# Pooled attention in groups of 128 and 16 instead of 72 and 72, tables split on the chip, and mixed planes stored twice

## The chip, the core and the metric

The kernel runs on one core of a Trainium2 chip. The metric is the time of one execution on the device in microseconds, the median of three runs. TensorE (PE in the rows, PEld for its weight loads) multiplies matrices, VectorE (DVE), ScalarE (ACT) and GpSimd (POOL) compute elementwise, and SyncE (SP) and GpSimd issue DMA transfers. All engines run their own list of instructions in order and wait for each other through semaphores.

## What is computed

Inputs are q, k, v of shape 8 x 8 x 576 x 64 (batch, heads, positions, width) and two weight matrices of 512 x 2048 and 2048 x 512.

```python
q_d, k_d, v_d = (x.reshape(B, H, 144, 4, D).mean(axis=3) for x in (q, k, v))
out_d = softmax_attention(q_d, k_d, v_d)                  # 144 groups of 4 positions
out_up = np.repeat(out_d, 4, axis=2)
mask = np.abs(pos[:, None] - pos[None, :]) < 4
out_local = masked_softmax_attention(q, k, v, mask)
x = (out_up + out_local) -> (8, 576, 512)
mixed = np.real(fft(fft(x, axis=1), axis=2))
u = x + mixed
un = (u - mean(u)) / sqrt(var(u) + 1e-6)
out = u + relu(un @ w_ch1) @ w_ch2
```

## The kernel before

**Order.** The kernel writes its order by hand. Each piece of work is put into a list with a due time, `at(t, fn)`; the list is sorted, and each engine gets its instructions in that order. The unit is the planner's own and no time on the chip: a batch is `PACE = 20` units, and the table `AT` holds the offsets of every step. An instruction that waits holds up everything behind it on its engine, and a DMA that waits for its source or its buffer holds up the transfers behind it in the queue of SyncE or GpSimd.

**Stages.** For each of the 8 batches: `Unit` is local attention over five pairs of 64-position windows; `Pooled` is attention over the 144 groups; `Mix` folds the result, multiplies it with the tables of cosines and sines (`seqm` along the positions, `chanm` along the channels) as a real Fourier transform, and stores the mixed planes in device memory (`um`). The pooled result goes to `ud`, the local one to `ul`. After the batches comes the feed-forward part: `Block` n takes 512 tokens, adds `ul`, `um` and `ud` into `ut`, normalises, transposes and multiplies with the weights (lines L832 and L850 to L852). The first blocks begin while the last batches are still in work. fp32r products are made from a high and a low part of an operand, three matmuls for one.

**Pooled attention before.** The 144 groups are two halves of 72 on 72 partitions (`GH`). A batch goes in four rounds of two heads; each round has the steps scores (`sp`, L322), maxima (`mxd`, L327), exponentials (`sd`, L338), transposes of 72x72 (`tp`, L348), copies out of PSUM (`ptd`, L359), values (`avd`, L367) and result (`odt`, L378 to L382). `sums` holds the summed q and k (L436 to L439), made from the loaded `qkT` (L419), of which there are six buffers for the five units of a batch. `vsum`, the sums of v, is loaded and then added to three times by DMA (L311). `move` (L391, L392) carries rows of the second half to where the fold wants them: 8 rows inside `odt` and 64 rows to the local result's slot 2; `store` writes `ud`.

**Tables and planes before.** `seqm` and `chanm` come from device memory as high and low part, one DMA each from GpSimd (L552, L555). The mixed planes are two per batch; a block adds them with one DMA for each half of the channels (L762). In `Mix`, `split_low` makes the low part of the folded input on GpSimd (`fl`, L600).

Of the kernel before, what the change touches and what calls it, by code (L numbers as in the profile page):

```python
# [19 lines left out]
POOL_BATCHES = (2,3,4,5,6,7)  # L20
EARLY_LOW = 1

# [8 lines left out]
    "sums": (-2.2, 0.17),  # L31
    "sum_v": (-14.47, -9.55, -2.25, 2.08),
    "load_v": (-2.02, 4.21),
    "store_pooled": (0.1, 0.68),
    "crosses": ((1, 4.04), (2, 6.77), (0, 9.29)),
    "folds": ((3, 4.1), (1, 4.66), (2, 8.37), (0, 10.52)),
    "splits": (0.74, 0.9, 1.86),
    "z": (9.34, 11.56, 13.39, 16.53),
    "sequence": (12.84, 1.74, 0.82, 1.64),
    "mixed": (21.92, 2.32, 0.48, 0.57, 1.73, 2.55),  # L40
    "store_local": (9.77,),
    "ffn": (2.28, 1.64),
    "decode": (49.28, 9.87, 4.65, 1.15, 1.87),
    "decode_steps": (-1.42, -0.6, 0.89, 2.11, 2.34),
    "add0": (61.1, 0.73, 5.8),
    "early": (5.46, 2.11),
    "constants": (17.38, 15.22, 23.31),
    "qk1": (-16.47, 3.41),
    "sum_v1": (-19.42, -12.25, -2.94, 2.36),
    "qk0": (-9.18, 1.93),  # L50
    "sums0": (-0.79, 0.34),
    "sums1": (-1.23, 0.3),
    "load_v0": (1.25, 5.23),
    "load_v1": (0.9, 3.69),
    "sum_v0": (-13.22, -6.45, -4.76, 5.84),
    "pairs0": (4.4, 5.57, 10.95, 11.33),
    "units0": (-2.86, -0.07, 6.22, 12.28, 17.42),
    "norms0": (87.98, -0.75, 94.54, 4.13),
    "add1": (78.83, 3.12, 14.11),
    "norms1": (127.29, 3.89, 1.92, 1.93),  # L60
    "keep": (23.57,),
    "shift": (-0.22,),
    "pace0": (0.95, 1.0),
# [5 lines left out]
ROUND = 5  # L69
TILES = 4  # L70
# [14 lines left out]
def kernel(  # L85
# [24 lines left out]
    GH = G // 2  # L110
# [4 lines left out]
    GX = G - W  # L115
# [14 lines left out]
    um = [dram.tile([2, NSL * P, HN1], F32, name=f"um{b}") for b in range(B)]  # L130
# [101 lines left out]

    odt = pd.tile([GX, 2, DM + 2], F32, name="odt")
    nc.gpsimd.memset(odt[:, :, 0:1], 0.0)
# [38 lines left out]
    for x in xab:  # L273
        nc.gpsimd.memset(x[:, :, :, 0:1], 0.0)
        nc.gpsimd.memset(x[W:, NSL - 1, 1, 1 : DM + 1], 0.0)
# [10 lines left out]
    def pooled_end(b):  # L286
        return pooled_at(b) + (15 if b else AT["pairs0"][3]) + pooled_pace(b) * AT["pooled_steps"][-1]
# [12 lines left out]
    class Pooled:  # L300
        def __init__(self, b):
            self.b = b
            self.sps, self.mx, self.sd, self.tps, self.pts, self.av = {}, {}, {}, {}, {}, {}

        def sum_v(self, r):

            if r == 0:
                self.vs = pd.tile([GH, 2, H, D + 1], F32, name="vsum", bufs=2)
            eng = nc.gpsimd if r else nc.sync
            how = {"accum_op": ALU.add} if r else {}  # L310
            eng.dma_start(out=self.vs.rearrange("g t h d -> g (t h d)"), in_=vg[self.b, r], **how)  # L311

        def scores(self, h0):
            s = sums[self.b]
            sps = self.sps[h0] = [
                bank("sp", GH)[:, : 2 * G].rearrange("p (a g) -> p a g", a=2) for _ in range(2)
            ]
            for t in range(2):
                for hl, sp in enumerate(sps):
                    r = slice(hl * D, hl * D + D)  # L320
                    qT = s[r, 0, h0 // 2, t * GH : (t + 1) * GH]
                    nc.tensor.matmul(sp[:, t, :], qT, s[r, 1, h0 // 2, :], start=True, stop=True)  # L322

        def maxima(self, h0):
            mx = self.mx[h0] = pd.tile([GH, 4], F32, name="mxd", bufs=2)
            for hl, sp in enumerate(self.sps[h0]):
                nc.vector.tensor_reduce(  # L327
                    out=mx[:, 2 * hl : 2 * hl + 2], in_=sp, axis=AX.X, op=ALU.max, negate=True
                )

        def exps(self, h0):
            mx = self.mx[h0]
            nc.scalar.mul(out=mx, in_=mx, mul=2.0**-7)
            sd = self.sd[h0] = pd.tile([GH, 4, G], F32, name="sd", bufs=1)
            for hl, sp in enumerate(self.sps[h0]):
                for t in range(2):
                    i = 2 * hl + t
                    nc.scalar.activation(  # L338
                        out=sd[:, i, :], in_=sp[:, t, :], func=AF.Exp, scale=2.0**-7, bias=mx[:, i : i + 1]
                    )  # L340

        def transpose_p(self, h0):
            self.tps[h0] = []
            for hl in range(2):
                tp = bank("tp", GH)[:, : 2 * G].rearrange("p (a g) -> p a g", a=2)
                for kt in range(2):
                    for t in range(2):
                        nc.tensor.transpose(  # L348
                            tp[:, kt, t * GH : (t + 1) * GH],
                            self.sd[h0][:, 2 * hl + t, kt * GH : (kt + 1) * GH],  # L350
                            ident[:GH, :GH],
                        )
                self.tps[h0].append(tp)

        def copy_p(self, h0):
            self.pts[h0] = []
            for tp in self.tps[h0]:
                pt = pd.tile([GH, 2, G], F32, name="ptd", bufs=NUM_PT)
                nc.scalar.copy(out=pt, in_=tp)  # L359
                self.pts[h0].append(pt)  # L360

        def values(self, h0):
            av = self.av[h0] = bank("avd", GH)[:, : 4 * (D + 1)].rearrange("p (t h d) -> p t h d", t=2, h=2)
            for hl in range(2):
                for t in range(2):
                    for kt in range(2):
                        nc.tensor.matmul(  # L367
                            av[:, t, hl, :],
                            self.pts[h0][hl][:, kt, t * GH : (t + 1) * GH],
                            self.vs[:, kt, h0 + hl, :],  # L370
                            start=(kt == 0),
                            stop=(kt == 1),
                        )

        def result(self, h0):
            av = self.av[h0]
            rs = pd.tile([GH, 2, 2], F32, name="rsd", bufs=2)
            nc.vector.tensor_scalar(  # L378
                out=rs, in0=av[:, :, :, D], scalar1=1e-9, scalar2=4.0, op0=ALU.add, op1=ALU.mult
            )  # L380
            nc.vector.reciprocal(out=rs, in_=rs)
            nc.vector.tensor_mul(  # L382
                out=odt[:GH, :, h0 * D + 1 : (h0 + 2) * D + 1].rearrange("g t (h d) -> g t h d", h=2),
                in0=av[:, :, :, 0:D],
# [742 lines left out]
```

## Time and profile before

| | us |
|---|---|
| median of three runs | 1140.27 (1137.82 to 1142.56) |
| profiled execution | 1141.05 |
| its span, first to last instruction | 1139.3 |
| TensorE busy | 1087.2 (95%) |
| VectorE busy | 513.5 (45%) |
| ScalarE busy | 352.2 (31%) |
| GpSimd busy | 348.0 (31%) |

The busy share is a mean over two different parts. Up to about 333 us the batches are in work and all engines take turns; behind that the feed-forward part runs. A view by stretches separates them. The chain that ended last follows the work back from the last instruction, at each step to what released it.

### The profile page before, as it was taken

The page shows a single profiled execution, that of the slowest core. Times are in us where ns is not written, and L with a number is a line of the kernel's source. Part 1 is how long each engine was busy: PE and PEld are TensorE (multiplying, and loading weights), DVE is VectorE, ACT ScalarE, POOL GpSimd, SP SyncE. Part 2 cuts the span into 40 slices and gives each one's busy share as a digit, 9 for nine tenths or more (in the row PEclk, how much of TensorE's full clock was granted, in tenths as well). Part 3 has the DMA queues.
Part 4 walks back from the last instruction along what each step waited for, and adds up shares of the span by engine and source line. Part 5 has one row for each costly group of instructions (what it writes and reads, how often), then busy time and mean ns, then how long its engine had stood idle before and what let it go on. Part 6 is the DMA issues. An engine that isn't in the chain of part 4 may idle for free.

```text
span 1139.3 us, 20899 instructions
## 1 busy us (share of the span) xinstructions
PE 1087.2 (95%) x8252; PEld 910.8 (80%) x8252; DVE 513.5 (45%) x1230; ACT 352.2 (31%) x1057; POOL 348.0 (31%) x509
## 2 busy tenths in 40 slices
PE   6899797999999899999999999999999999999998
PEld 4787686788978687888888888888888888888887
DVE  4877788779769887132322222222232222132111
ACT  4777565767744443111111111111111111111110
POOL 2346857645364564405003004102201300400000
PEclk7899798889999999999999999999999999999999
DMA  8968989977354442706106005203302401500001
GB/s 265 305 165 259 260 195 261 224 207 201 120 171 125 120 129 66 148 1 131 17 1 134 15 1 111 38 1 97 52 1 78 71 1 56 93 1 34 4 1 37
DMA packets 64195, 119.45 MB, mean 105 GB/s; under 512 B 8573, under 2 KB 22669, under 8 KB 63842
## 3 DMA queue, kind: packets, MB, share of 16 engines
q1 hardware_dynamic: 44850, 87.57, 24.4%
q0 software_dynamic: 19248, 30.56, 15.8%
q8 instruction: 65, 1.06, 0.4%
q14 instruction: 32, 0.26, 0.1%
HBM read 89.86 MB, written 27.05 MB: 103 GB/s over the span
## 4 chain that ended last, share of the span: by engine, by line
PE 73%; DVE 9%; DMA 7%; ACT 5%; POOL 3%; issue 2%; SPq 0%; DVEq 0%; ACTq 0%; POOLq 0%
PE hps L832 30%; PE acc L852 10%; PE acc L850 10%; PE acc L851 10%; DMA raw<-in_wq_dram 3%; DMA qkT<-in_qk_dram 3%; PE y L620 3%; PE mix L666 2%; ACT sb L473 1%; PE avd L367 1%; DVE sums L439 1%; DVE x L521 1%; PE tpn L800 1%; PE av L502 1%; PE sc L454 1%
## 5 line engine op out<-in xcount | busy, mean ns | idle before, releaser
L840 DVE SCALAR_TENSOR_TENSOR hl<-hps,hh 128x512 fp32r<-128x512 f32 x144 | 99.5, 691 | 481.1 <-ACT hh L836 481.1
L832 PE MATMUL hps<-unT,w1h 128*128 128x512 f32 x1152 | 311.1, 392 | 0.0
L832 PEld LDWEIGHTS hps<-unT,w1h 128*128 128x128 f32 x1152 | 214.2, 188 | 43.2
L836 ACT ACTIVATE hh<-hps 128x512 fp32r<-128x512 f32 x144 | 86.0, 597 | 523.6 <-PE hps L832 523.6
L850 PE MATMUL acc<-w2h,hh 128*128 128x512 f32 x576 | 225.5, 391 | 3.1 <-DVE ut L856 2.9
L852 PE MATMUL acc<-w2h,hl 128*128 128x512 f32 x576 | 225.3, 391 | 0.0
L851 PE MATMUL acc<-w2l,hh 128*128 128x512 f32 x576 | 224.6, 390 | 0.0
L832 PE MATMUL hps<-unT,w1l 128*128 128x512 f32 x576 | 154.3, 390 | 0.0
L762 POOL DMA_DIRECT2D ut<-um x96 | 84.1, 1518 | 205.6 <-DMA ut<-ul 172.6
L850 PEld LDWEIGHTS acc<-w2h,hh 128*128 128x128 f32 x576 | 108.4, 188 | 27.1 <-ACT w1h L211 2.0
L852 PEld LDWEIGHTS acc<-w2h,hl 128*128 128x128 f32 x576 | 108.5, 188 | 23.9 <-DVE hl L840 1.3
L832 PEld LDWEIGHTS hps<-unT,w1l 128*128 128x128 f32 x576 | 108.2, 188 | 23.0
L851 PEld LDWEIGHTS acc<-w2l,hh 128*128 128x128 f32 x576 | 108.4, 188 | 22.2
L785 POOL TENSOR_TENSOR rstd<-rstd,mhalf 128x1 f32<-128x1 f32 x36 | 20.1, 558 | 267.5 <-DVE rstd L784 261.7
L473 ACT ACTIVATE sb<-sc,mx 128x64 f32<-128x64 f32 x320 | 70.0, 330 | 1.3
L600 POOL TENSOR_TENSOR fl<-xeo,fh 128x512 fp32r<-128x512 f32 (+1 forms) x32 | 44.1, 1386 | 25.1 <-ACT fh L593 20.2
L809 DVE TENSOR_TENSOR unT<-tpn,unT 128x512 fp32r<-128x512 f32 x36 | 24.8, 690 | 59.0 <-ACT unT L806 59.0
L620 PE MATMUL y<-seqm,fh 128*128 128x290 f32 (+1 forms) x256 | 44.6, 315 | 5.7 <-ACT fh L593 4.2
L181 ACT ACTIVATE wt<-raw 128x256 f32<-128x256 f32 x64 | 28.2, 441 | 64.7 <-DMA raw<-in_wq_dram 47.5
L575 POOL TENSOR_TENSOR pq<-x 128x256 f32<-128x256 f32 x48 | 30.6, 671 | 56.6 <-DVE x L521 47.7
L759 POOL DMA_DIRECT2D ut<-ud x40 | 46.1, 1911 | 2.0 <-DMA ut<-um 1.1
L620 PEld LDWEIGHTS y<-seqm,fh 128*128 128x128 f32 (+1 forms) x256 | 37.4, 197 | 8.8 <-ACT fh L593 5.2
(97 smaller groups left out, 1346.4 us busy)
## 6 DMA issues: line engine op xcount, KB each, us to landing
qkT<-in_qk_dram SPq DMA_DIRECT2D x40, 512.0 KB
raw<-in_wq_dram SPq DMA_DIRECT2D x64, 256.0 KB
vaug<-in_vw_dram SPq DMA_DIRECT2D x40, 260.0 KB
out_dram<-ut SPq DMA_DIRECT2D x36, 256.0 KB
ul<-x SPq DMA_DIRECT2D x8, 1024.0 KB
ut<-ud POOLq DMA_DIRECT2D x32, 256.0 KB, 6.5
vsum<-in_vg_dram POOLq DMA_DIRECT2D x24, 292.5 KB, 7.1
ut<-um POOLq DMA_DIRECT2D x48, 128.0 KB, 4.4
```

The source lines that it names most:

```text
L473: nc.scalar.activation(out=self.sb[:, hp, h2], in_=sc[:, hp], func=AF.Exp, scale=0.125, bias=self.mx[:, h2, hp : hp + 1],)
L575: nc.gpsimd.tensor_tensor(out=pq[:, i], in0=u[:, t, HD + 1 : DM + 1], in1=v[:, t, 0:HD], op=ALU.add)
L600: nc.gpsimd.tensor_sub(out=l, in0=self.x[t], in1=h.bitcast(F32))
L620: nc.tensor.matmul(y, l, r, start=(i == 0), stop=(i == len(mms) - 1))
L759: nc.gpsimd.dma_start(out=u[to : to + m], in_=groups, accum_op=ALU.add)
L762: nc.gpsimd.dma_start(out=u[to : to + m, h * HD : h * HD + HD], in_=um[b][i, k + j : k + j + m, z : z + HD], accum_op=ALU.add,)
L832: nc.tensor.matmul(hps, a[:, c, :], unT[:, x, c, :], start=(i == 0), stop=(i == len(mms) - 1))
L836: nc.scalar.activation(out=hh, in_=self.hps[f], func=AF.Relu)
L840: nc.vector.scalar_tensor_tensor(out=hl, in0=self.hps[f], scalar=0.0, in1=self.hh[f].bitcast(F32), op0=ALU.max, op1=ALU.subtract)
L850: nc.tensor.matmul(acc, hh, w2h, start=start, stop=False)
L851: nc.tensor.matmul(acc, hh, w2l, start=False, stop=False)
L852: nc.tensor.matmul(acc, hl, w2h, start=False, stop=stop)
```

## The change

Pooled attention works on 128 groups and 16 left over. A batch has three parts: part 0 takes the 16 left over of all eight heads at once, as 32-row strips (16 of them other groups that are computed again), parts 1 and 2 take the 128 groups of four heads each. The sums of v carry two more columns of heads with the rows left over, and `spread` copies them on ScalarE into `vds`, zero elsewhere. The result of the 128 groups lies where the fold reads it; the 16 rows left over go to slot 2 of the local result by four small DMAs, and from there to `ud`.

The tables come as plain words in eight pieces through SyncE, into the still unused `ut` tiles; ScalarE makes the high part and VectorE the low part. For batches 0 and 1 three planes are stored, one of them twice, so that one DMA adds both halves of the channels. The low part of fold slot 0 and two small operations of `split_z` go from GpSimd to VectorE. Nearly every offset of the order is another; the lines below show those of the steps named here.

```diff
 AT = {
-    "pooled": (1.17, -0.12, -1.81, -2.91, -3.5),
-    "mix": (19.06, 17.6, 18.05),
-    "local_steps": (0, 1.57, 2.24, 4.76, 5.59, 7.9, 9.26),
-    "pooled_steps": (0.66, 1.79, 2.89, 4.92, 5.63, 7.66, 8.86),
-    "qk": (-12.1, 2.19),
-    "sum_v": (-14.47, -9.55, -2.25, 2.08),
-    "store_pooled": (0.1, 0.68),
+    "pooled": (1.39, -0.67, -3.4, -4.0, -3.53),
+    "mix": (18.69, 18.25, 18.08),
+    "local_steps": (0.47, 2.18, 2.55, 4.76, 5.66, 7.44, 8.16),
+    "pooled_steps": (0.21, 1.79, 2.89, 4.92, 5.63, 7.66, 9.61),
+    "qk": (-14.26, 2.19),
+    "sum_v": (-14.82, -12.57, -2.25, 2.01),
+    "store_pooled": (1.06, 1.34, 3.47),
...
-    "constants": (17.38, 15.22, 23.31),
-    "sum_v1": (-19.42, -12.25, -2.94, 2.36),
-    "norms1": (127.29, 3.89, 1.92, 1.93),
-    "shift": (-0.22,),
+    "constants": (10.75, 29.61),
+    "waves": ((16.5, 0.16), (17.55, 0.92), (21.37, 0.9)),
+    "waves_c": ((21.38, -3.88), (23.72, -0.25), (25.94, 6.11)),
+    "sum_v1": (-19.42, -12.25, -4.44, 3.9),
+    "norms1": (146.64, 3.89, 0.79, 1.85),
+    "shift": (0.5,),
+    "parts": (0.22, 5.36, 9.32),
+    "spread": (11.49, 5.0),
...
-    um = [dram.tile([2, NSL * P, HN1], F32, name=f"um{b}") for b in range(B)]
+    um = [dram.tile([4 if b < TWICE else 2, NSL * P, HN1], F32, name=f"um{b}") for b in range(B)]
...
-                self.vs = pd.tile([GH, 2, H, D + 1], F32, name="vsum", bufs=2)
+                self.vs = pd.tile([P, H + 2, D + 1], F32, name="vsum", bufs=2)
...
+        def spread(self):
+            for k in range(4):
+                r = slice(k * LQ, k * LQ + LQ)
+                nc.scalar.copy(out=vds[self.b % 2][r, :, k % 2], in_=self.vs[r, H:])
+
+        def scores(self, i):
...
+            for a in range(2 if i else HP):
+                for hl, sp in enumerate(sps):
+                    r = slice(hl * D, hl * D + D)
+                    if i:
+                        hp = 2 * i - 2 + a
+                        nc.tensor.matmul(sp[:, a, :], s[r, 0, hp, :P], s[r, 1, hp, :], start=True, stop=True)
+                    else:
+                        nc.tensor.matmul(
+                            sp[a * LQ : a * LQ + LQ, 0, :], s[r, 0, a, G - LQ :], s[r, 1, a, :], start=True, stop=True
+                        )
...
+        def transpose_p(self, i):
+            sd, n = self.sd[i], self.sps[i][0].shape[1]
+            main, rest = (bank("tp")[:, : m * P].rearrange("p (m q) -> p m q", q=P) for m in (2 * n, 1))
+            for a in range(n):
+                for hl in range(2):
+                    nc.tensor.transpose(main[:, 2 * a + hl, :], sd[:, a, hl, :P], ident)
+            for k in range(4):
+                x = sd[:, k % 2 if i else 0, k // 2, G - LQ :]
+                nc.tensor.matmul(rest[k * LQ : k * LQ + LQ, 0], x, ident, start=True, stop=True)
...
+        def values(self, i):
...
+            for a in range(1 if i else HP):
+                for hl, o in enumerate(av):
+                    r = slice(hl * D, hl * D + D)
+                    q = slice(0, P) if i else slice(a * LQ, a * LQ + LQ)
+                    v = vd[r, i - 1] if i else vd[r, a // 2, a % 2]
+                    nc.tensor.matmul(
+                        o.rearrange("p a d -> p (a d)") if i else o[q, 0, :],
+                        rest[r, 0, q],
...
+            for a in range(2 if i else HP):
+                for hl, o in enumerate(av):
+                    hp = 2 * i - 2 + a if i else a
+                    q = slice(0, P) if i else slice(a * LQ, a * LQ + LQ)
+                    nc.tensor.matmul(
+                        o[:, a, :] if i else o[q, 0, :],
+                        main[:, 2 * a + hl if i else hl, q],
+                        self.vs[:, 2 * hp + hl, :],
...
         def move(self):
             x = xab[self.b % 2]
-            STORE.dma_start(out=odt[GH:GX, 0, 1 : DM + 1], in_=odt[W:GH, 1, 1 : DM + 1])
-            STORE.dma_start(out=x[W:, NSL - 1, 0, 1 : DM + 1], in_=odt[:W, 1, 1 : DM + 1])
+            for hp in range(HP):
+                STORE.dma_start(
+                    out=x[W : W + GL, NSL - 1, 0, 1 + hp * P : 1 + hp * P + P],
+                    in_=self.rest[(hp + 1) * LQ - GL : (hp + 1) * LQ],
+                )
+
+        def store_rest(self):
+            STORE.dma_start(out=ud[self.b][P:], in_=xab[self.b % 2][W : W + GL, NSL - 1, 0, 1 : DM + 1])
...
-    def sequence_waves():
-        nc.gpsimd.dma_start(out=seqm, in_=c_seq)
...
+    def load_waves(k):
+        nc.sync.dma_start(out=waves[k][1], in_=waves[k][0])
+
+    def waves_high(k):
+        nc.scalar.copy(out=waves[k][2], in_=waves[k][1])
+
+    def waves_low(k):
+        nc.vector.tensor_sub(out=waves[k][3], in0=waves[k][1], in1=waves[k][2].bitcast(F32))
...
-            nc.gpsimd.tensor_sub(out=l, in0=self.x[t], in1=h.bitcast(F32))
+            eng = nc.vector if t in LOW_ON_VECTOR else nc.gpsimd
+            eng.tensor_sub(out=l, in0=self.x[t], in1=h.bitcast(F32))
...
+                elif part and b < TWICE:
...
+                    nc.gpsimd.dma_start(
+                        out=u[to : to + m].rearrange("p (h c) -> p h c", h=2),
+                        in_=planes.rearrange("h (r c) -> r h c", c=HN1)[:, :, :HD],
+                        accum_op=ALU.add,
+                    )
```

## Rows read from the trace of the kernel before

**Rows 1.** Busy us of each engine by stretch, with granted clock, DMA share, GB/s.
```profile
core 0: us, PE busy (x) PEld busy (x) DVE busy (x) ACT busy (x) POOL busy (x), PEclk, DMA share, GB/s
16.00:333.00 317.00, 280.71 (x4550) 245.34 (x4551) 242.46 (x719) 208.19 (x766) 171.11 (x261) 0.91 0.79 219
20.00:40.00 20.00, 19.25 (x391) 15.42 (x388) 15.29 (x47) 13.83 (x55) 5.18 (x7) 0.88 0.97 297
...
400.00:1000.00 600.00, 599.90 (x2690) 495.45 (x2690) 177.55 (x332) 94.81 (x178) 135.65 (x177) 1.00 0.27 59
```

**Rows 2.** Chain that ended last, 16 to 333 us, share of the stretch by line.
```profile
by line: PE y L620 9.1%; DMA qkT<-in_qk_dram 7.6%; ACT sb L473 5.2%; PE avd L367 5.1%; PE mix L666 5.0%; DVE sums L439 4.9%; DVE x L521 4.9%; PE av L502 4.4%; issue 4.1%; PE sc L454 3.5%; PE sp L322 2.9%; PE tpl L485 2.9%; PE tp L348 2.6%; 
```

**Rows 3.** TensorE in order of time: start us, us, engine, line, operation, count.
```profile
281.17 0.60 PE L485 MATMUL tpl<-ident,sb 128*128 128x128 f32 x4
281.60 0.67 PE L348 MATMUL tp<-ident,sd 72*72 72x72 f32 x8
282.20 0.71 PE L322 MATMUL sp<-sums 64*72 64x144 f32 x8
282.84 0.51 PE L666 MATMUL mix<-chanm,yh 128*128 128x258 f32 x2
...
284.27 0.29 PE L666 MATMUL mix<-chanm,yl 128*128 128x258 f32 x1
284.40 0.28 PE L666 MATMUL mix<-signs,yz 128*128 128x258 f32 x1
284.61 0.70 PE L502 MATMUL av<-vaug,pT 64*64 64x65 f32 x32
...
285.80 1.25 PE L367 MATMUL avd<-vsum,ptd 72*72 72x65 f32 x16
286.87 0.43 PE L666 MATMUL mix<-chanm,yh 128*67 128x258 f32 x2
```

**Rows 4.** Chain over the whole span, single pieces: start us, us, what.
```profile
59.45 6.51 DMA qkT<-in_qk_dram
...
81.31 2.15 DMA odt<-odt
...
184.71 8.02 DMA qkT<-in_qk_dram
...
227.57 9.49 DMA qkT<-in_qk_dram
```

**Rows 5.** Chain, 117 to 141.3 us, share of the stretch by line.
```profile
by line: POOL ut L762 28.0%; DMA odt<-odt 13.7%; POOL fl L600 9.1%; PE avd L367 7.8%; ACT sb L473 7.2%; PE mix L666 6.5%; issue 4.6%; PE tpl L485 3.6%; DVE o L678 3.2%; DVE xeo L586 3.1%; PE y L620 2.5%; ACT pT L493 2.4%; ACT fh L593 2.1%; 
```

**Rows 6.** Groups by line and form up to 345 us: count, busy us, mean ns.
```profile
L338 ACT ACTIVATE sd<-sp,mxd 72x144 f32<-72x144 f32 x128 | 37.9, 373 | 1.4 <-PE tp L348 0.4
L600 POOL TENSOR_TENSOR fl<-xeo,fh 128x512 fp32r<-128x512 f32 x24 | 34.1, 1424 | 7.9 <-ACT fh L593 6.7 <-DMA qkT<-in_qk_dram 1.0
...
L327 DVE TENSOR_REDUCE mxd<-sp 72x2 f32<-72x288 f32 x64 | 26.0, 445 | 10.0 <-PE sp L322 10.0
...
L762 POOL DMA_DIRECT2D ut<-um x22 | 20.1, 1362 | 0.3 <-DMA vaug<-in_vw_dram 0.2
...
L809 DVE TENSOR_TENSOR unT<-tpn,unT 128x512 fp32r<-128x512 f32 x5 | 3.4, 686 | 3.8 <-ACT unT L806 3.8
```

**Rows 7.** Chain that ended last, share of the span by engine, from the page.
```profile
PE 73%; DVE 9%; DMA 7%; ACT 5%; POOL 3%; issue 2%; SPq 0%; DVEq 0%; ACTq 0%; POOLq 0%
```

**Rows 8.** Busy time of each engine over the span, from the page.
```profile
PE 1087.2 (95%) x8252; PEld 910.8 (80%) x8252; DVE 513.5 (45%) x1230; ACT 352.2 (31%) x1057; POOL 348.0 (31%) x509
```

**Rows 9.** DMA issues of the tables: KB each, us to landing.
```profile
seqm<-in_c_seq_dram POOLq DMA_DIRECT2D x1, 2320.0 KB, 12.2
...
chanm<-in_c_chan_dram POOLq DMA_DIRECT2D x1, 1032.0 KB, 11.6
```

**Rows 10.** Line L391, the moves: count, duration ns, first and last start us.
```profile
L391 SPq DMA_DIRECT2D odt<-odt x8: 698/704/767, 42.9 to 309.6; - x8
```

**Rows 11.** Line L311, additions of vsum, from issue to landing.
```profile
DMA to landing us min/median/max: 4.7/7.1/11.1
```

More of the change, by code (lines that the diff above doesn't have):

```diff
@@ L231 @@
     pd = p1.enter_context(tc.tile_pool(name="pd", bufs=1, side="right"))
-    odt = pd.tile([GX, 2, DM + 2], F32, name="odt")
-    nc.gpsimd.memset(odt[:, :, 0:1], 0.0)
+    odt = pd.tile([P, DM + 2], F32, name="odt")
+    nc.gpsimd.memset(odt[:, 0:1], 0.0)
+    vds = [pd.tile([P, 2, 2, D + 1], F32, name=f"vd{i}") for i in range(2)]
+    for x in vds:
+        nc.gpsimd.memset(x, 0.0)
     pbank = ExitStack()
@@ L331, in exps @@
[L331 to L373, printed above, removed]
@@ new lines, in result @@
+        def result(self, i):
+            av = self.av[i]
+            n = av[0].shape[1]
+            rs = pd.tile([P, 2, 2], F32, name="rsd", bufs=2)[:, :, :n]
+            for hl, o in enumerate(av):
+                nc.vector.tensor_scalar(
+                    out=rs[:, hl], in0=o[:, :, D], scalar1=1e-9, scalar2=4.0, op0=ALU.add, op1=ALU.mult
+                )
+            nc.vector.reciprocal(out=rs, in_=rs)
+            if i:
+                to = odt[:, 1 + (i - 1) * 4 * D : 1 + i * 4 * D]
+            else:
+                to = self.rest = pd.tile([P, 2 * D], F32, name="rest", bufs=1)
+            to = to.rearrange("p (a h d) -> p a h d", h=2, d=D)
+            for hl, o in enumerate(av):
+                nc.vector.tensor_mul(
+                    out=to[:, :, hl], in0=o[:, :, 0:D], in1=rs[:, hl].unsqueeze(2).to_broadcast([P, n, D])
+                )
@@ L581, in fold @@
             if t < NSL:
-                a, b = self.pq[t][:, 0], self.pq[t][:, 1]
+                a, b = (self.pq[t][: rows[t], i] for i in range(2))
             else:
-                a, b = odt[:, 0, HD + 1 : DM + 1], odt[:, 0, 0:HD]
+                a, b = odt[:, HD + 1 : DM + 1], odt[:, 0:HD]
             nc.vector.tensor_add(out=x[:, 0:HD], in0=a, in1=b)
@@ L594, in split_high @@
             if t == NSL:
-                nc.scalar.copy(out=zf[:n, t], in_=odt[:, 0, HD : HD + 1])
+                nc.scalar.copy(out=zf[:n, t], in_=odt[:, HD : HD + 1])
         def split_low(self, t):
@@ L886 @@
         u.plan()
-    for t, fn in zip(AT["constants"], (sequence_waves, channel_waves, clear_yz)):
+    for t, fn in zip(AT["constants"], (load_signs, clear_yz)):
         at(t, fn)
+    for k in range(len(waves)):
+        for (first, step), fn in zip(AT["waves" if k < 5 else "waves_c"], (load_waves, waves_high, waves_low)):
+            at(first + step * (k if k < 5 else k - 5), fn, k)
     last = mix_at(B - 1)
@@ L1013, in _constants @@
         seq[rows, 1, m // 2] = sn
[L1015 to L1025 removed]
+    g = np.arange(S // 4)
+    g = np.where(g < S // 8, g, S // 4 - 1 - (g - S // 8))
+    group = np.zeros((2, S // 4, len(k1)))
+    for r in range(4):
+        group += np.stack(waves(4 * g + r))
+    seq[:, :, 3] = group[:, :P].transpose(1, 0, 2)
+    seq[W : W + S // 4 - P, :, 2] = group[:, P:].transpose(1, 0, 2)
+    seq = seq.reshape(P, -1)
     j = np.arange(DM // 2 + 2)
```

218 lines of the change are left out of this document (122 added, 96 removed).

## Prediction

> **What bounds the kernel now.** I read the page first, then the busy time by stretch, then the chain that ended last, and last the single rows of the instructions that the change removes or adds. The span is 1139.3 us and the profiled execution took 1141.05, so 1.75 us lie outside the span. From 400 to 1000 us TensorE is busy 599.90 of 600 us at full clock [rows 1]: that is the feed-forward part, which the change does not touch, so it can only start earlier or later. What can move is the 317 us from 16 to 333. There TensorE is busy 280.71 us (89%), VectorE 242.46, ScalarE 208.19, the granted clock averages 0.91 of 2.4 GHz, and the DMA engines are busy 0.79 of the time, 0.97 from 20 to 40 us at 297 GB/s [rows 1]. No engine is full; the work goes from engine to engine. The chain confirms it: in that stretch its largest items are the sequence matmuls (9.1%), the landing of qkT (7.6%), the exponentials (5.2%) and the pooled value matmuls (5.1%) [rows 2]. The reader is to see that an instruction saved is worth its share on the chain, and its whole time only where its engine is what everybody waits for.
>
> **TensorE.** Durations are steps between starts in a stretch that keeps TensorE busy at full clock [rows 3]: four transposes of 128x128 take 0.43 us (0.108 each), eight pooled transposes of 72x72 take 0.60 (0.075), eight pooled scores 0.64 (0.080), sixteen pooled values 1.07 (0.067). A batch has 32, 32 and 64 of them: 2.56 + 2.40 + 4.29 = 9.25 us. After, a batch has 16 score matmuls (8 with 128 stationary columns, 8 with 32), 10 transposes of 128x128, 12 plain matmuls against the identity and 28 value matmuls (12 with 128 stationary columns, 16 with 32). No row shows these shapes. I price the wide ones, the transposes and the plain matmuls as the 128x128 transpose (0.108), the narrow scores at 0.080 and the narrow values at 0.067: scores 0.86 + 0.64, transposes 1.08 + 1.30, values 1.30 + 1.07, together 6.25 us. That saves 3.0 us a batch, 24 us in all. If the narrow ones run four at a time, as the 64x64 local matmuls seem to (32 of them begin and end within 0.70 us), the 24 narrow ones cost about 0.02 each and the plain ones 0.067: 4.5 us a batch, 38 us saved. The low end: the three lines hold 5.1 + 2.9 + 2.6 = 10.6% of the chain's 317 us, 33.6 us [rows 2], of which 3.0/9.25 is 10.9. TensorE is at 89%, so the truth lies between chain share and full price; I take the middle of 10.9 and 24, **-17**.
>
> The new code asks for more kinds of tiles: per part the transposes go from full height to 32-column pieces and the values from half height to full. The row shows what such a step costs: within the mix group one matmul follows another after 0.13 us, the first 64x64 matmul after it comes 0.21 us later [rows 3], so 0.08 more. With 2 more steps a part, 6 a batch, 48 in all, that is about 4 us; at the same share as above (17 of 24) **+3**. The Trainium skill (TensorEngine Tiling (Array Packing), Tiling Modes, Key Properties) says that changing the tiling mode drains TensorE. If a drain is the part of a matmul's record that its successor normally hides, 0.28 - 0.13 = 0.15 us [rows 3], 48 of them are 7.2 us in place of 3, and the sum below would be 4 us worse; the row of 0.08 speaks for less.
>
> **The moved rows.** Before, 8 rows of odt go to itself and 64 rows to x by DMA once the last pair of heads is done, and the fold of the group slot waits for them. On the chain this landing stands twice: 2.15 us [rows 4] and 13.7% of 24.3 = 3.33 us [rows 5]. After, slot 3 is read where the result was written, and the 16 rows left over go out after the first part, two parts before they could hold anything up. What is late next is the fold itself, which waited for nothing else. **-5.5**; at worst the second landing finds another cover and it is -2.
>
> **The mixed planes.** In 117 to 141.3 us the additions of um fill 28.0% of the chain, 6.8 us [rows 5]: GpSimd issues them (1.362 us each, 22 up to 345 us, all of batches 0 and 1 [rows 6]) and the low parts of the sequence input stand behind them. After, one DMA carries both halves, so 11 are issued. If an issue costs as before the half is saved, **-3.4**; if it costs double, because it names twice the pieces, nothing; if the rest moves off the chain too, 6.8.
>
> **VectorE, ScalarE, GpSimd.** VectorE gets the low part of slot 0 (8 at 0.686, the price of a subtraction of that size [rows 6]) 5.5 us, eight table subtractions of at most that price, 5.5, and sixteen tiny z operations, which no row here prices, between nothing and the 0.445 of a 72x288 reduction; I take 0.2, so 3.2. The maxima go from 64 at 0.445 to 32 of that width and 16 of half of it (0.33, between half price and full): 28.5 to 19.5. The normalisations are more but smaller (15 against 12 a batch): nothing. Net +5.2 us. ScalarE loses 48 exponentials at 0.373 [rows 6], 17.9 us; its 8 table copies and 32 spread copies stand against a quarter fewer copies out of PSUM and fewer scalings: nothing net. GpSimd loses 8 subtractions at 1.424 [rows 6], 11.4 us. Shares: the chain spends 9, 5 and 3% of the span on these engines [rows 7], 102.5, 57 and 34 us, over busy times of 513.5, 352.2 and 348.0 [rows 8]: 0.20, 0.16 and 0.10. So +1.0 - 2.9 - 1.1 = **-3.0**.
>
> **Bytes.** The tables were 2320 and 1032 KB [rows 9]; half of that, 1.72 MB, goes away in the stretch in which DMA is full, 5.8 us at 297 GB/s. The group sums of v grow from 292.5 to 325 KB, 32 times, 1.06 MB over the whole stretch; two planes more are 0.6 MB; the moves fall by 0.9 MB. I take **-2**, between 0 and -6.
>
> **Two waits that the new order makes.** A batch is 20 units of the order; the eight moves run from 42.9 to 309.6 us [rows 10], 38.1 us a batch, 1.9 us a unit.
> First, qkT. On the chain its landing takes 6.51, 8.02 and 9.49 us [rows 4]. The load of the next batch's last unit needs the buffer that the local scores of unit 3 free, so it cannot start sooner. From those scores to the next batch's pooled scores the order has 5.16 units (9.8 us) before and 4.21 (8.0 us) after for batches 4 to 7, 5.75 and 3.74 for batch 3, 6.85 and 4.34 for batch 2: 8.3 units, 15.8 us less in all. That bounds the loss from nothing to 15.8; behind the waiting scores stand the local matmuls on TensorE. I take **+5**, as three landings in seven stood on the chain.
> Second, the spread. ScalarE now copies rows of vsum 2.99 units (5.7 us) after its last addition is issued, 1.1 units (2.1 us) in batch 1; the first reader used to come 5.58 units after. An addition lands after 7.1 us in the median, 4.7 at least and 11.1 at most [rows 11]. So 1.4 us in six batches and 5.0 in batch 1, 13.5 us of ScalarE, with the local exponentials and copies queued behind. At ScalarE's share that is 2.2; **+3**. The table copies wait for plain loads issued units earlier; I cost that at nothing, covered by the exponentials before them, and 3 us if the first loads are late.
>
> **Sum.** -17 + 3 - 5.5 - 3.4 - 3.0 - 2 + 5 + 3 = -19.9. From the profiled execution's 1141.05 that is 1121.2; the median of the runs is 0.8 lower, 1140.27, so **1120 us**.
>
> **The rivals.**
> TensorE is the limit after all: clock 0.91 and 89% busy speak for it, the chain's mixed engines against. Then -30 (between 24 and 38) + 3 - 5.5 - 6.8 - 3 - 6 = -48, **1092**.
> The time saved comes back as the wait for qkT: for it, that scores now stand 1 to 2.5 units nearer to the loads; against it, that four batches show no such landing on the chain. With TensorE at its low end and the um DMAs at double price: -10.9 + 3 - 5.5 - 3 - 2 + 3 + 15.8 = +0.4, **1140**, no change; so too if the change simply lies off the path.
> Slower: ScalarE stands at the spread until vsum has landed. If additions land as late as the latest, 11.1 us, six batches stand 5.4 us and batch 1 9.0: 41 us, all on the path because the local exponentials are behind. Against the sum without its +3: -22.9 + 41 = +18, **1158**. It decides from about 3.3 us a batch on (22.9 over 7), that is, when landings come later than 9.0 us; the median of 7.1 speaks against it.
>
> **How the numbers follow.** Chances: the sum 0.55 (own range 1108 to 1133), TensorE the limit 0.13, qkT or off the path 0.19, the spread 0.13. A difference of 0.5% (5.7 us) is about what a measurement of this kernel can tell from none. Faster: 0.55 + 0.13 and 0.02 of the qkT case, 0.70. Same: 0.16 of that case. Slower: the spread's 0.13 and 0.01 of the qkT case, 0.14. The range 1097 to 1145 leaves out most of the case of 1092 (0.09) and of 1158 (0.11).
>
> **What the profile after would show.** Right: the feed-forward part as long as now and starting about 20 us sooner; no landing of odt on the chain; the three pooled TensorE lines down from 10.6% of the stretch to 7; half as many um additions and no stretch like 117 to 141 us; TensorE's idle time in 16 to 333 us not above today's 36 us. Wrong: ScalarE waiting at the spread for vsum by more than 3 us a batch, landings of qkT in every batch, plain identity matmuls well above 0.108 us, or a feed-forward part that starts earlier and then waits for its weights, since their decoding starts only when the local buffers close.

## The result, and the profile after

The kernel after the change takes 1125.43 us (median, 1123.41 to 1127.43) where the one before took 1141.41 in the same comparison: a ratio of 0.9864, interval 0.9832 to 0.9896, so 16 us or 1.4% faster. The forecast was 1120 with a range of 1097 to 1145. The total is close. The experiments show that most of the terms behind it are not.

The profiled execution took 1124.34 us. First the page: the busy time of each engine, and the chain that ended last by engine.

```profile
PE 1065.8 (95%) x8204; PEld 880.6 (78%) x8204; DVE 519.7 (46%) x1270; ACT 349.2 (31%) x1025; POOL 330.5 (29%) x473
...
PE 78%; DMA 8%; DVE 6%; ACT 4%; issue 2%; POOL 1%; SPq 0%; POOLq 0%; ACTq 0%; DVEq 0%
```

Next the busy time by stretch. The columns are those of [rows 1]; 316.72 us is where the first matmul of the second weight matrix starts (line L931, tile `acc`; L850 before, at 328.46).

```profile
16.00:316.72 300.72, 258.98 (x4489) 213.22 (x4490) 243.39 (x752) 201.71 (x729) 149.37 (x219) 0.93 0.81 225
20.00:40.00 20.00, 14.26 (x334) 10.59 (x326) 15.02 (x49) 13.47 (x50) 3.19 (x4) 0.93 0.90 238
140.00:160.00 20.00, 10.23 (x169) 8.40 (x168) 9.96 (x35) 6.62 (x24) 6.20 (x11) 0.74 0.96 239
317.00:389.00 72.00, 69.61 (x329) 57.29 (x328) 64.69 (x131) 33.07 (x84) 41.28 (x66) 1.00 0.44 127
400.00:1000.00 600.00, 600.00 (x2698) 496.49 (x2697) 171.94 (x318) 91.50 (x165) 126.91 (x162) 1.00 0.26 55
```

The same view of before, cut at its own first `acc` matmul:

```profile
16.00:328.46 312.46, 276.18 (x4525) 241.28 (x4526) 238.89 (x710) 205.58 (x758) 168.59 (x257) 0.91 0.80 221
```

That is 312.46 us with TensorE busy 276.18 at a mean granted clock of 0.91. So the span's 16.7 us (1139.3 to 1122.6) fall apart like this: 11.7 us before that matmul and 5.0 after it (810.8 to 805.9). In the first part TensorE is busy 17.2 us less and idle 5.4 us more (41.7 against 36.3). Not all of the 17.2 us is work that is gone, since the same matmuls are busy for longer at a lower clock: the experiment "Only z on GpSimd" below has the same 4489 records and is busy 268.33 us at a mean clock of 0.90. Busy time multiplied by the mean clock is 276.18 x 0.91 = 251 us before and 258.98 x 0.93 = 241 after. By this estimate, good to some 2 us because the clock has two digits, about 10 us are matmuls saved and about 7 are the higher clock. New holes have opened: 20 to 40 us had 19.25 busy [rows 1] and has 14.26; 140 to 160 us has 10.23, at a mean clock of 0.74, so partly at the lower of the two levels, 1.2 GHz.

Of the 5 us behind the first `acc` matmul some 3.5 can be named. Before, 14 sequence matmul records still stood there, now 2: twelve at 0.145 us, 1.7 us. The first 72 us ran at a mean clock of 0.98 and now run at 1.00: 1.4 us. TensorE's idle time from the first `acc` matmul to the end fell from 6.9 to 6.5 us.

The chain from 16 to 318 us, shares by line and then single pieces (start us, us, what), answers to [rows 2, 4, 5].

```profile
by line: DMA raw<-in_wq_dram 11.3%; DMA vsum<-in_vg_dram 8.8%; PE y L686 7.7%; issue 4.9%; ACT sb L525 4.5%; PE mix L732 4.5%; DMA qkT<-in_qk_dram 3.8%; PE tpl L537 3.6%; PE avd L406 3.5%; PE sc L506 2.9%; PE av L554 2.3%; DMA vaug<-in_vw_d
...
21.02 7.06 DMA vsum<-in_vg_dram
...
43.80 5.00 DMA vsum<-in_vg_dram
...
68.61 7.16 DMA vsum<-in_vg_dram
...
100.88 8.41 DMA raw<-in_wq_dram
...
135.54 17.94 DMA raw<-in_wq_dram
...
185.84 7.87 DMA raw<-in_wq_dram
...
219.41 6.89 DMA qkT<-in_qk_dram
```

The reader is to see three things. No landing of `odt` is left, as forecast. The landing of `qkT`, on which the forecast put 5 us, went from 24.0 [rows 4] to 3.8% of 302 = 11.5 us. And the largest item is one that the forecast did not have: the weights' raw words (`raw`), 34.1 us of the chain (11.3%), one piece of it 17.94 us long.

The groups up to 345 us (columns as in [rows 6]):

```profile
L360 ACT ACTIVATE sd<-sp,mxd 128x144 f32<-128x144 f32 x80 | 24.4, 381 | 0.8
...
L836 POOL DMA_DIRECT2D ut<-um x11 | 13.7, 1583 | 0.3
...
L342 PE MATMUL sp<-sums 64*128 64x144 f32 x128 | 12.7, 317 | 0.0
...
L330 ACT COPY vd<-vsum 32x130 f32<-32x130 f32 x32 | 9.5, 298 | 2.3 <-DMA vsum<-in_vg_dram 2.0
...
L666 DVE TENSOR_TENSOR fl<-xeo,fh 128x512 fp32r<-128x512 f32 x8 | 6.5, 815 | 0.8 <-ACT fh L658 0.7
...
L675 DVE TENSOR_TENSOR z<-zf,z 128x4 fp32r<-128x4 f32 x8 | 3.4, 424 | 2.7 <-ACT z L674 2.7
```

The waits from 16 to 318 us (who, for what: us in all, times, longest):

```profile
ACT wt L187 <- DMA raw<-in_wq_dram: 14.7, 5, 8.7
...
ACT z L674 <- DVE zf L671: 5.8, 5, 3.4
...
PE yz L710 <- DVE z L675: 4.8, 4, 2.0
...
ACT vd L330 <- DMA vsum<-in_vg_dram: 2.0, 3, 1.5
```

On VectorE slot 0's low part takes 0.815 us (forecast 0.686) and the subtraction of `split_z` 0.424 (forecast 0.2). The spread, on which the slower rival rested, makes ScalarE wait 2.0 us in all; the forecast had 13.5. The additions of `um` are halved, 22 to 11, at 1.583 us in place of 1.362. The longest wait for raw words and what stands behind it, in order of time:

```profile
153.50 0.43 ACT L187 ACTIVATE wt<-raw 128x256 f32<-128x256 f32 x1 [8.66 <-DMA raw<-in_wq_dram]
...
155.04 0.80 PE L732 MATMUL mix<-chanm,yh 128*128 128x258 f32 x2 [9.09 <-ACT sb L525]
```

ScalarE stands 8.66 us at a word that isn't there; the local exponentials (`sb`, L525) are behind it in its list, and TensorE stands 9.09 us for them. That is the hole at 140 to 160 us.

### The profile page after: what moved, and what is told of

Read it like the earlier page. It is cut to its first block, busy times and chain, and to the rows that moved or that the text cites. A ratio compares the mean times of both kernels' runs of the same rounds, so it can differ in the third digit from the quotient of the medians.

```text
span 1122.6 us, 20797 instructions
## 1 busy us (share of the span) xinstructions
PE 1065.8 (95%) x8204; PEld 880.6 (78%) x8204; DVE 519.7 (46%) x1270; ACT 349.2 (31%) x1025; POOL 330.5 (29%) x473
## 4 chain that ended last, share of the span: by engine, by line
PE 78%; DMA 8%; DVE 6%; ACT 4%; issue 2%; POOL 1%; SPq 0%; POOLq 0%; ACTq 0%; DVEq 0%
PE hps L913 34%; PE acc L931 11%; PE acc L933 11%; PE acc L932 11%; DMA vsum<-in_vg_dram 3%; DMA raw<-in_wq_dram 3%; PE y L686 2%; PE mix L732 2%; ACT sb L525 1%; PE tpn L881 1%; DMA qkT<-in_qk_dram 1%; PE tpl L537 1%; PE avd L406 1%; PE sc L506 1%; PE av L554 1%
## 5 line engine op out<-in xcount | busy, mean ns | idle before, releaser
L931 PE MATMUL acc<-w2h,hh 128*128 128x512 f32 x576 | 224.7, 390 | 2.0 <-DVE ut L937 2.0
L931 PEld LDWEIGHTS acc<-w2h,hh 128*128 128x128 f32 x576 | 108.0, 188 | 25.4 <-DVE ut L937 2.0
L843 POOL DMA_DIRECT2D ut<-um x72 | 62.1, 1538 | 195.7 <-DMA ut<-ul 162.5
L525 ACT ACTIVATE sb<-sc,mx 128x64 f32<-128x64 f32 x320 | 70.0, 330 | 1.3
L732 PE MATMUL mix<-chanm,yh 128*128 128x258 f32 (+1 forms) x160 | 34.4, 310 | 13.8 <-ACT sb L525 11.1
L887 ACT CAST unT<-tpn 128x512 fp32r<-128x512 f32 x36 | 21.2, 588 | 76.8 <-PE tpn L881 76.8
L192 POOL TENSOR_SCALAR wt<-wt 128x256 f32<-128x256 f32 x64 | 31.7, 496 | 35.3 <-ACT mx L522 14.1
L206 DVE SCALAR_TENSOR_TENSOR wt<-raw,wt 128x256 int32<-128x256 int32 x64 | 40.5, 633 | 2.2
```

What stands on the lines that cost most here:

```text
L206: nc.vector.scalar_tensor_tensor(out=t, in0=self.lo, scalar=29, in1=t, op0=ALU.logical_shift_right, op1=ALU.bitwise_or)
L525: nc.scalar.activation(out=self.sb[:, hp, h2], in_=sc[:, hp], func=AF.Exp, scale=0.125, bias=self.mx[:, h2, hp : hp + 1],)
L732: nc.tensor.matmul(to, l, r, start=(i == 0), stop=(i == len(mms) - 1))
L843: nc.gpsimd.dma_start(out=u[to : to + m, h * HD : h * HD + HD], in_=um[b][i, k + j : k + j + m, z : z + HD], accum_op=ALU.add,)
L931: nc.tensor.matmul(acc, hh, w2h, start=start, stop=False)
```

## The experiments

All ratios are to the kernel before, which ran in each comparison again (medians of 1139.18 to 1141.49 us); they can differ by up to 0.0017 from the quotient of the two medians. The first two questions: did the total come from TensorE, and which of the small edits count?

**Planes once** (after, without the doubled planes).

```diff
-TWICE = 2
+TWICE = 0
```

> The changed kernel, with two planes per batch again and two additions for each piece (the order is not touched). Theory A, the parts add up as forecast: 3.4 us slower than the changed kernel (between 0 and 6.8), so about 1129 us, and GpSimd issues 22 additions up to 345 us in place of 11. Theory B, the pooled attention and the order bring everything: within 2 us of the changed kernel, since GpSimd was not what the others waited for.

1125.9 us, 0.986 (0.9838 to 0.9882). The doubled planes can't be told from nothing here, nor from the forecast 3.4 us: a difference below some 4 us lies within these intervals.

**Tables by GpSimd** (after, tables as high and low part again, by one DMA each).

```diff
-        nc.sync.dma_start(out=waves[k][1], in_=waves[k][0])
...
+        nc.gpsimd.dma_start(out=seqm, in_=c_seq)
...
+        nc.gpsimd.dma_start(out=chanm, in_=c_chan)
```

> The changed kernel, with the tables coming as high and low part by one DMA each from GpSimd, at the offsets they had before. Theory A: 1.72 MB more in a stretch in which DMA is full, against 8 pieces less on ScalarE and on VectorE: 1 us slower (between 3 faster and 5 slower). Theory B: within 2 us. A third view: the DMA engines are the limit up to 60 us, then all of 5.8 us comes back, 1131 us.

1126.07 us, 0.986 (0.9838 to 0.9882). The saved bytes can't be told from nothing either.

**Low parts on GpSimd** (after, slot 0's low part and both operations of `split_z` back).

```diff
-LOW_ON_VECTOR = (0,)
+LOW_ON_VECTOR = ()
...
-            nc.vector.tensor_tensor(
+            nc.gpsimd.tensor_tensor(
...
-            nc.vector.tensor_sub(out=z[:, :, 1:2], in0=zf, in1=z[:, :, 0:1].bitcast(F32))
+            nc.gpsimd.tensor_sub(out=z[:, :, 1:2], in0=zf, in1=z[:, :, 0:1].bitcast(F32))
```

> The changed kernel, with the low part of fold slot 0 and the two small z operations on GpSimd again. Theory A: nothing that can be measured, since 11.4 us less on GpSimd at its chain share of 0.10 and 8.7 us more on VectorE at 0.20 cancel. Rival: GpSimd's queue stands in front of the sequence matmuls, then 8 times 0.7 us or more come back, 1131 us or above.

1135.91 us, 0.9956 (0.9933 to 0.998): 10 us lost, the first edit that counts. Its waits from 16 to 333 us offer two causes, `vsum` at the spread and `z` at TensorE:

```profile
ACT vd L330 <- DMA vsum<-in_vg_dram: 11.2, 6, 3.2
...
PE yz L710 <- POOL z L675: 10.2, 6, 2.5
```

**Weights earlier** (after, decoding planned 2 units earlier).

```diff
-    "decode": (50.58, 9.93, 4.05, 1.15, 1.87),
+    "decode": (50.58, 9.93, 6.05, 1.15, 1.87),
```

> The changed kernel, with the fetch of the weight quarters that are decoded during the batches 2 units earlier. Theory D: a wait is new in the changed kernel, ScalarE for the weights' raw words, 18.2 us in all and 8.7 at the longest, with TensorE idle for 9.1 us behind it, because the fetch stands 2.71 units (5 us) ahead of its first reader where it stood 3.23. Then an earlier fetch takes most of it away: 5 to 10 us faster, 1115 to 1120, and no wait of ScalarE for raw above 3 us. Rival: the DMA engines are full there, so the fetch lands as late or something else lands later in its place: within 2 us.

1122.39 us, 0.983 (0.9808 to 0.9852): the lowest median of the study, 3 us below the kernel after, though the two intervals overlap. ScalarE's wait for raw words falls from 14.7 to 4.8 us, the longest from 8.7 to 1.8. But other landings stand on the chain in its place, one of them here:

```profile
144.63 10.81 DMA vsum<-in_vg_dram
```

So the hole is closed in part (from 140 to 160 us TensorE is busy 14.29 us, in place of 10.23) and in part exchanged: the DMA engines are full there in both kernels (share 0.96, now 1.00), the words come sooner, and the sums of v stand on the chain in their place.

**Pooled alone** (the edits of the first three together, so that of the change only the pooled part, the moves and the order stay).

> The changed kernel, with two planes, the tables by GpSimd, and the low part of slot 0 and z on GpSimd, all three at once: what is left of the change is the pooled attention in 128 and 16, and the order. Theory A, the parts add up: 1125.4 + 3.4 + 1 = about 1130 us, 11 faster than before. Theory B, pooled attention and order bring everything: about 1125 us. If the three together hide a loss of the pooled part: 1138 or above.

1139.03 us, 1.0016 (0.9991 to 1.0041). Without the three small edits the change gains nothing. Its busy time by stretch, up to its own first `acc` matmul:

```profile
16.00:327.61 311.61, 270.24 (x4489) 220.51 (x4490) 225.62 (x721) 197.96 (x721) 168.31 (x256) 0.89 0.78 221
```

By the estimate above the matmuls are saved here too (270.24 x 0.89 = 241, as in the kernel after, against 251). A lower clock, 0.89 against 0.91, and 41.4 us of idle time against 36.3 take the saving back.

**Half the values, before** (the kernel before, with the second half of the value matmuls left out).

```diff
-                    for kt in range(2):
...
+                    nc.tensor.matmul(
+                        av[:, t, hl, :],
+                        self.pts[h0][hl][:, 0, t * GH : (t + 1) * GH],
```

> The kernel before, with half of the pooled value matmuls left out (the second half of the groups is not added, so the output is not the reference's): 32 of 64 instructions of 0.067 us a batch, 17 us of TensorE in all, and nothing else changed. It prices a microsecond of TensorE. Chain share: half of the 16.2 us that the line has on the chain, 8 us faster, 1133. TensorE as the limit: 17 us faster, 1124. Others are the limit: within 2 us.

1138.95 us, 0.9998 (0.9978 to 1.0018). Its busy time by stretch, up to its own first `acc` matmul:

```profile
16.00:325.50 309.50, 261.18 (x4269) 223.02 (x4270) 235.32 (x707) 205.85 (x758) 168.43 (x257) 0.91 0.80 223
```

TensorE is busy 15.0 us less than in the same stretch of before (276.18), and idle 12.0 us more (48.3 against 36.3). TensorE's time alone buys nothing in the old order.

**Planes twice, before** (the old kernel with the doubled planes alone).

```diff
-    um = [dram.tile([2, NSL * P, HN1], F32, name=f"um{b}") for b in range(B)]
+    um = [dram.tile([4 if b < TWICE else 2, NSL * P, HN1], F32, name=f"um{b}") for b in range(B)]
```

> The kernel before, with only the three planes of batches 0 and 1 and one addition for both halves. Theory A: 3.4 us faster (between 0 and 6.8), 1138, with the stretch of 117 to 141 us shorter. Theory B: within 2 us, because what stands behind the additions on GpSimd waits for something else next.

1147.62 us, 1.0084 (1.0056 to 1.0111), slower. A landing of `qkT` of 13.93 us stands on the chain where the kernel before had none; whether it is the cause was not tried:

```profile
144.33 13.93 DMA qkT<-in_qk_dram
```

**Scores doubled** (after, each wide pooled score matmul twice; a repeat overwrites the first).

```diff
-                        nc.tensor.matmul(sp[:, a, :], s[r, 0, hp, :P], s[r, 1, hp, :], start=True, stop=True)
+                        for _ in range(2):
+                            nc.tensor.matmul(sp[:, a, :], s[r, 0, hp, :P], s[r, 1, hp, :], start=True, stop=True)
```

> The changed kernel, with the wide pooled score matmuls issued twice (the second writes the same result): 16 instructions of 0.087 us more a batch, 11 us of TensorE in all. TensorE as the limit: 11 us slower, 1136. Chain share: the line has 2.5 us on the chain, so 2 to 4 us slower, 1128 to 1129. Others are the limit: within 2 us.

1129.44 us, 0.9923 (0.9904 to 0.9942), so 0.0059 of 1141, 6.7 us, above the kernel after, for 11 us of matmuls: 0.6 us for each. Saving in the old order gave nothing, adding in the new costs more than half. The price of a microsecond of TensorE depends on what else is late.

**Low parts on VectorE, before** (the reverse of the third experiment, in the old kernel).

```diff
-            nc.gpsimd.tensor_sub(out=l, in0=self.x[t], in1=h.bitcast(F32))
+            eng = nc.gpsimd if t else nc.vector
+            eng.tensor_sub(out=l, in0=self.x[t], in1=h.bitcast(F32))
```

and both operations of `split_z` as in the change.

> The kernel before, with only the low part of fold slot 0 and the two small z operations on VectorE. Putting them back on GpSimd cost the changed kernel 10 us. Theory F: that is so because GpSimd's last addition of vsum stands behind them and ScalarE and TensorE now wait for it at the spread; the kernel before reads vsum 5.58 units after that addition is issued, so it gains little: within 3 us, 1137 to 1143. Rival: GpSimd in front of the sequence matmuls was a bound of the kernel before as well: 7 to 11 us faster, 1129 to 1133.

1150.46 us, 1.007 (1.0043 to 1.0097): 8 us slower. What the new order needs hurts the old one. Its TensorE waits 8.4 us for low parts on VectorE, where the kernel before waits 4.7 for those on GpSimd, and VectorE waits 9.9 us for ScalarE between the two operations of `split_z`; whether these are the cause was not tried.

**Low parts on GpSimd, sums early** (the third experiment again, with the last additions of `vsum` issued sooner, to tell its two waits apart).

```diff
-    "sum_v": (-14.82, -12.57, -2.25, 2.01),
+    "sum_v": (-14.82, -12.57, -7.0, -2.3),
```

> The kernel with the low part of slot 0 and z on GpSimd again (1135.9 us), in which the third and the last addition of vsum are issued 4.75 and 4.31 units earlier, in front of the sums of q and k. Theory F: the 10 us were the wait for vsum at the spread (11.2 us of ScalarE's idle time), so most of it comes back: 1126 to 1130, and ScalarE's idle time at the spread falls below 3 us. Rival: the 10 us are the sequence matmuls' wait for low parts and z on GpSimd, 21 us of idle time before the z matmuls: then 1133 or above.

1137.86 us, 0.9971 (0.9947 to 0.9996). Its waits, 16 to 333 us:

```profile
PE yz L710 <- POOL z L675: 12.8, 6, 4.2
...
ACT vd L330 <- DMA vsum<-in_vg_dram: 1.2, 2, 1.1
```

The wait at the spread went from 11.2 to 1.2 us and the time did not come back: that cause fell. `z` and slot 0's low part are left.

**Only z on GpSimd** (after, only the two operations of `split_z` back; slot 0's low part stays on VectorE).

```diff
-            nc.vector.tensor_tensor(
+            nc.gpsimd.tensor_tensor(
...
-            nc.vector.tensor_sub(out=z[:, :, 1:2], in0=zf, in1=z[:, :, 0:1].bitcast(F32))
+            nc.gpsimd.tensor_sub(out=z[:, :, 1:2], in0=zf, in1=z[:, :, 0:1].bitcast(F32))
```

> The changed kernel, with only the two small z operations on GpSimd, the low part of slot 0 stays on VectorE. Theory F (the low part of 1.4 us in front of the additions of vsum is what costs): within 3 us of the changed kernel. Rival (the z operations wait in GpSimd's queue and TensorE for them): 5 to 10 us slower, 1130 to 1135.

1136.26 us, 0.9946 (0.9925 to 0.9967). The whole loss of the third experiment is in sixteen operations of 0.2 us. One of them in order of time, first GpSimd's list and then TensorE's:

```profile
214.54 1.22 POOL L640 TENSOR_TENSOR pq<-x 128x256 f32<-128x256 f32 x2 [0.75 <-DVE xeo L651]
215.73 0.19 POOL L671 TENSOR_TENSOR zf<-x 128x3 f32<-128x3 f32 x1
216.23 0.20 POOL L675 TENSOR_TENSOR z<-zf,z 128x4 fp32r<-128x4 f32 x1 [0.30 <-ACT z L674]
```

```profile
216.48 1.24 PE L710 MATMUL yz<-seqm,z 128*2 128x290 f32 x8 [1.37 <-POOL z L675]
```

Its waits from 16 to 318 us, and behind them its busy time up to its first `acc` matmul:

```profile
ACT z L674 <- POOL zf L671: 16.7, 8, 4.8
...
PE yz L710 <- POOL z L675: 13.9, 7, 3.4
```

```profile
16.00:328.62 312.62, 268.33 (x4489) 219.32 (x4490) 236.67 (x738) 201.55 (x729) 154.69 (x235) 0.90 0.77 217
```

`z` stands behind the fold's additions (`pq`) on GpSimd, and TensorE waits for it 13.9 us in place of 4.8. ScalarE, which makes the high part of `z`, waits longer too, 16.7 us for `zf` in place of 5.8; the runs don't separate the two waits. The change of order is the likely reason why this matters now, though no run moves it back: in the kernel before, also with `z` on GpSimd, TensorE waits for it only 1.6 us. There the matmuls of `z` stood 2.22 units behind `split_z` (9.34 and 11.56 in the table of offsets), and now they stand 0.71 behind it (9.21 and 9.92). The 9.1 us of wait do not all add to TensorE's idle time, which is 44.3 against 41.7 us (other waits are shorter); the stretch is 11.9 us longer because it is also busy 9.4 us more, at a mean clock of 0.90 against 0.93, more of it at 1.2 GHz. That the waits are what lowered the clock is likely, since TensorE loses both together, but no run separates them.

**Weights and sums early** (the fourth experiment with the sums of the tenth).

> The changed kernel, with the weights fetched 2 units earlier (that alone: 1122.4) and the third and last addition of vsum 4.75 and 4.31 units earlier. If vsum is still late at places in the changed kernel (8.7% of its chain), 3 to 8 us faster than with the weights alone: 1115 to 1119. If ScalarE's 2.0 us of idle time at the spread are all that vsum costs, within 2 us of 1122.4.

1125.18 us, 0.9859 (0.983 to 0.9888): no further gain. `vsum` moves away from the one place and back in at another (127.10 us, 11.85 long), and a landing of `ut` from `ud` of 7.77 us joins it.

## Why the prediction was right and its reasons were not

**TensorE, -17.** The term was mis-sized. I counted the kernel before by the trace's records and the kernel after by the code's matmuls, and these differ: a plain f32 matmul stands as two records, a transpose as one. The group of the wide scores (L342) shows it, 128 records for the 64 matmuls of eight batches. After the change a batch has 32 records of scores, 34 of transposes and identity matmuls and 56 of values. At the forecast's prices (74 at 0.108, 16 at 0.080, 32 at 0.067) these would cost 11.4 us a batch, more than the 9.25 of before; what they do cost is in the rows below, TensorE in order of time at full clock (columns as in [rows 3]).

```profile
262.01 0.48 PE L344 MATMUL sp<-sums 64*32 64x144 f32 x16
262.48 1.32 PE L686 MATMUL y<-seqm,fh 128*128 128x290 f32 x8
...
268.13 0.38 PE L369 MATMUL tp<-ident,sd 128*128 128x128 f32 x2
268.44 0.43 PE L372 MATMUL tp<-ident,sd 128*32 128x128 f32 x8
268.80 0.76 PE L342 MATMUL sp<-sums 64*128 64x144 f32 x8
269.49 0.51 PE L732 MATMUL mix<-chanm,yh 128*128 128x258 f32 x2
...
271.88 0.41 PE L393 MATMUL avd<-vd,ptd 64*32 64x65 f32 x16
272.23 0.46 PE L406 MATMUL avd<-vsum,ptd 128*32 128x65 f32 x16
272.61 0.30 PE L500 MATMUL sc<-maskb,identb 64*64 64x256 bf16 x2
...
274.80 0.60 PE L537 MATMUL tpl<-ident,sb 128*128 128x128 f32 x4
275.16 0.48 PE L732 MATMUL mix<-chanm,yh 128*67 128x258 f32 x2
...
276.84 0.66 PE L369 MATMUL tp<-ident,sd 128*128 128x128 f32 x4
277.43 0.43 PE L372 MATMUL tp<-ident,sd 128*32 128x128 f32 x8
...
281.38 0.49 PE L393 MATMUL avd<-vd,ptd 64*128 64x130 f32 x4
281.80 1.11 PE L406 MATMUL avd<-vsum,ptd 128*128 128x65 f32 x8
282.75 0.61 PE L369 MATMUL tp<-ident,sd 128*128 128x128 f32 x4
283.28 0.42 PE L372 MATMUL tp<-ident,sd 128*32 128x128 f32 x8
```

Steps from start to start: scores 0.47 + 2 x 0.69, transposes 0.31 + 2 x 0.59, identity matmuls 3 x 0.36, values 0.35 + 0.38 + 2 x (0.42 + 0.95); 7.89 us a batch. That saves 1.36 a batch, 10.9 us in all, where 24 was forecast; the estimate from busy time and clock gave about 10. Two errors worked against each other: there are more records, and the narrow ones are far cheaper, 0.02 to 0.045 us each. What the saving is worth is a second question. The forecast put its price between chain share and full; half the values left out of the old kernel gave nothing, the doubled scores in the new one cost 0.6 of their time. TensorE as the limit (1092) is excluded by the first of these.

**Tile modes, +3.** The size was about right at full price, though not the count. Four transposes between other full-size matmuls take 0.36 us (274.80 to 275.16), so 0.09 each; the same four with the 32-column matmuls behind them take 0.53 (282.75 to 283.28), or 0.59 where half-height scores stand in front as well (276.84 to 277.43). The step costs 0.17 us there, and behind two transposes 0.31 - 2 x 0.09 = 0.13. One such step a part makes some 0.47 us a batch, 3.8 in all, where the forecast had 48 steps at 0.08, 4 us; the steps within the values can't be told apart. All of this is already in the 7.89. The Trainium skill (TensorEngine Tiling (Array Packing), Tiling Modes, Key Properties) says that a change of mode drains the engine; the trace agrees with the 0.15 us that the forecast worked out for the rule, by 0.13 to 0.17 at this step; the 0.08 that it took instead is from another step, into 64x64 matmuls [rows 3].

**odt, -5.5.** The landing is gone from the chain, as forecast. That it was worth 5.5 us isn't shown: the pooled part with its moves and the new order, alone, gains nothing.

**Planes -3.4, bytes -2.** The issues were halved and the bytes saved, and undoing either can't be told from nothing; effects as small as those forecast are not refuted by that. Yet undoing them together with the low parts (1.0016) gives more time than the low parts alone (0.9956), and these intervals do not overlap. So both together are worth some 7 us by the ratios (0.006 x 1140), 3 by the medians alone, while GpSimd also has `z` to do. All three put work on GpSimd, which is the likely reason, but no run shows it.

**VectorE, ScalarE, GpSimd, -3.0.** This is the step that failed. The two operations of `split_z` were entered as 3.2 us of cost on VectorE, 0.6 us at the chain's share of 0.20. Their place decides, not their length: in the new order, which pulls the `z` matmuls forward, moving them carries 0.0082 x 1141 = 9.4 of the 16 us (5 to 14 by the two intervals). Slot 0's low part was entered as 11.4 us off GpSimd and 5.5 onto VectorE, 1.1 us of the chain each way, so as nothing; putting it back as well changes 0.9946 to 0.9956, which is nothing that can be told. ScalarE's part was mis-sized as well: 17.9 us less busy were forecast, -2.9 in the sum, and it is 3.0 less (352.2 to 349.2). The exponentials fell by 13.5 and not 17.9 (37.9 [rows 6] to 24.4; the forecast's price of 0.373 is the mean of records that overlap), and the spread alone adds 9.5. I had read that GpSimd's list is long, but not which of its instructions somebody was about to wait for.

**The two new waits, +5 and +3.** Neither cost what was put on it. `qkT` on the chain halved. Its loads are also planned 2.16 units sooner (-12.1 to -14.26 in the table of offsets), which the forecast set aside because the last unit's load waits for its buffer; whether that is why wasn't tried. The spread's wait is there, but small: three landings of `vsum`, 19.2 us (21.02, 43.80 and 68.61), end at the spread's first copy on a chain that had none of `vsum` before, yet they keep ScalarE waiting only 2.0 us in all. Issuing the additions sooner gained nothing on top of the earlier weights (1125.18 against 1122.39). The wait that did come, for raw words, was named only as weights that are late in the feed-forward part; it appears among the batches. Removing it gives about 3 us and lets others in.

**The rival of the other side** (1158, ScalarE at the spread) did not happen; nor did the return of all the gain as a wait for `qkT` (1140). But the pooled change without its small edits does end at no change, by another way than that rival: its TensorE waits 8.6 us for `z` and its ScalarE 9.1 us at the spread, and of these the tenth experiment shows that the second alone is not what costs.

**What was luck.** The forecast was right in that the feed-forward part only starts sooner, that `odt` leaves the chain and that the `um` additions are halved. The close total is luck, because errors cancelled. TensorE saved half of what was forecast, its idle time rose to 41.7 us where the forecast named 36 as the most, and raw words came late. Against that, the two new waits cost little of their 8 us. The order also made room for a wait for `z` that the forecast did not name, some 9 us, and it was the move to VectorE, entered as a small loss, that kept it out.

**What stays open.** How much pooled attention brings by itself in an order made for it: `z` on VectorE with planes and tables undone together was not run, and the old order can't carry the new parts. The hole at 20 to 40 us was not tried either, and 1.5 of the 5 us behind the first `acc` matmul have no name.

## What to carry to other kernels

Where several engines share a bound, cost a moved operation by who waits for it in the new order, not by its length: sixteen operations of 0.2 to 0.4 us carried some 9 of the 16 us, while the saved bytes and the halved issues, undone one at a time, could not be told from nothing. Try each edit undone from the new kernel and done alone in the old one; here two that help or cost nothing in the new one made the old one slower by 0.7 and 0.8%, so parts of a change that was ordered as a whole do not add up. Count both kernels in the same unit, records or matmuls, before multiplying by a price. And read a busy time together with the clock: of 17 us less, some 7 were only the higher clock.

## What the hardware showed that I had not expected

An f32 matmul of 128x128 against the identity with only 32 stationary columns steps in 0.36/8 = 0.045 us a record, a transpose of 128x128 in 0.36/4 = 0.09, and the step from these transposes to those matmuls adds 0.13 to 0.17 us. Values with 32 stationary columns step in 0.022 to 0.024 us, with 128 in 0.119. One DMA for both halves takes GpSimd 1.583 us to issue, against 1.362 for one half, so not twice. A landing of raw words took 17.94 us at a DMA share of 0.96, and 8.41 and 7.87 us elsewhere in the same stretch.
